# Ordering the fifth attention unit and two weight packets behind the first block's input

## Chip, cores and metric

One core of one Trainium2 chip runs the whole program. The metric is the device time of one execution in microseconds (us). TensorE (PE) does matrix products, VectorE (DVE), ScalarE (ACT) and GpSimd (POOL) work on elements, and SyncE (SP) issues most of the DMAs. Each engine works through its own instructions in a fixed order, which a scheduler has chosen when the program was built.

## What is computed

An attention with a forget gate over 4 batches, 8 heads, 576 positions and head size 64, and then two MLPs over its 2304 rows of 512, with 2048 hidden columns. All is float32; inside, most operands are split into a high part and a rest, and a product takes three terms.

```python
scores = q @ k.T / 8 + minimum(-(cum[:, None] - cum[None, :]), 0)   # cum = cumsum(maximum(s, 0))
attn = softmax(where(causal, -1e9, scores))
x = attn @ v                                       # heads side by side: (2304, 512)
x = (s * maximum(x @ w_in, 0)**2 + b) @ w_out      # first MLP
h = x @ w_in2
out = (maximum(h, 0) + alpha * minimum(h, 0)) @ w_out2
```

## The kernel before

The attention is cut into 32 units: a batch, a pair of heads, and a range of rows (0 to 319 or 320 to 575). `units` lists, for each batch, the four pairs of the first range and then the four of the second. Units 0 to 3 (`EARLY = 4`) have tiles of their own in places that weights take later. For a unit, `transpose_qk` turns q and k on VectorE (L375); `scores(u, h)` writes the bias of the gates for a head (L435 on VectorE; in the first eight units L431 on ScalarE for the second head), multiplies (sc, L457), adds and takes the minimum (L461), takes the exponential with its sum (L473), adds 1e-9 to the sum (L480), takes the reciprocal (L481) and normalizes on GpSimd (probs, L484). `values(u, h)` transposes the probabilities on TensorE (pt, L515), copies them (pf, L519), multiplies with v (av, L531) and copies the result into x (xf, L546).

The MLPs go over blocks of 256 rows (later ones of 512). A block has 16 steps `f`: `up(f)` makes 128 hidden columns (hp, L772), ScalarE and GpSimd apply the activation (L791, L793, L131), and `down(f)` adds to the block's output (acc, L886). Block 0 of the first MLP takes rows 0 to 255, so it needs units 0 to 3; `inputs(0, 0)` splits its x into xh (cast, L130) and xl (subtraction on VectorE, L131), four pieces each. In the first block the weights are made as it goes: `fetch(0, f)` loads a slice of w_in and w_out by DMA, and `packet(0, f)` brings its 64-bit numbers into float32 (`convert`: L140 on ScalarE, L141 and L142 on VectorE, for wi and for wo) and splits them (L130 on ScalarE; L131 on VectorE for the first, on GpSimd for the second). Packets 0 to 2 stand among the early units, packet 3 behind the scores of unit 2, and packet `f + 4` is asked for at step f (`AHEAD = 4`). The raw slices go into tiles that are used in turn: packet 6 takes those of packet 3, packet 7 those of packet 4.

`attention()` is a generator: each `next` writes a bit more of the attention into the program, in an order written out by hand. Before the block, the main loop calls it until `done` has reached the fourth unit, and at each step as far as `pace` says. The order of the program gives the priorities by which the scheduler, which runs a timeline of its own, fixes the order on each engine: an instruction that stands later may come first if its operands are ready earlier. `tc.issue_after(ins)` takes that freedom away: what is written inside it on the engine of `ins` comes behind `ins` on that engine.

`busy(n)` (L97) issues n products over zeros, 512 columns each, whose result is not used: 16 at the beginning, 1 after each of the early scores and values, and 4 at three places.

Of the kernel before, what the change touches and what calls it, by code (L numbers as in the profile page):

```python
# [8 lines left out]
F32 = mybir.dt.float32  # L9
# [4 lines left out]
ALU = mybir.AluOpType  # L14
# [5 lines left out]
def tile_forget_attention__then__two_mlps(  # L20
# [20 lines left out]
    nc = tc.nc  # L41
# [52 lines left out]
    def busy(n):  # L94

        for _ in range(n):
            tc.keep_in_program_order(nc.tensor.matmul(scratch, dense[:, :P], dense, start=True, stop=True))  # L97

    busy(16)
# [29 lines left out]
    def split(hi, lo, src, lo_eng=nc.vector):  # L129
        nc.scalar.copy(hi, src)  # L130
        lo_eng.tensor_tensor(out=lo, in0=src, in1=hi.bitcast(F32), op=ALU.subtract)  # L131
# [125 lines left out]
    xf = {}  # L257
# [111 lines left out]
    def transpose_qk(u):  # L369
# [4 lines left out]
        for dst, src in zip(turned, u.nats):  # L374
            nc.vector.transpose(dst, src)  # L375
# [28 lines left out]
    def scores(u, h):  # L404
# [11 lines left out]
        for r in u.blocks:  # L416
# [13 lines left out]
            if flip:  # L430
                nc.scalar.activation(  # L431
                    pt[:rows, :i1], u.cums[h][:rows, :i1], AF.Relu, scale=-1.0, bias=cumT[:rows, r, head : head + 1]
                )
            else:
                nc.vector.tensor_scalar(  # L435
                    out=pt[:rows, :i1], in0=u.cums[h][:rows, :i1], scalar1=cumT[:rows, r, head : head + 1],
                    scalar2=0.0, op0=ALU.subtract, op1=ALU.min,
                )
# [42 lines left out]
        nc.vector.reciprocal(sm[:, :nr], sm[:, :nr])  # L481
# [8 lines left out]
    def values(u, h):  # L490
# [45 lines left out]
        if u.n < EARLY:  # L536
            busy(4 if (u.n, h) == (EARLY - 1, 0) else 1)
# [24 lines left out]
    done = 0  # L562

    def attention():
# [33 lines left out]
        packet(0, 3)  # L598
        yield from alternate(scores(us[3], 0), values(us[2], 0), transpose_qk(u))
        yield from alternate(scores(us[3], 1), values(us[2], 1))  # L600
        yield from values(us[3], 0)
        last = us[3]
        for n in range(EARLY, len(units)):
# [3 lines left out]
            yield from alternate(scores(u, 0), values(last, 1))  # L607
# [22 lines left out]
    def inputs(layer, t):  # L630
# [20 lines left out]
        for c in range(NCC):  # L651
            on_pool = layer == 0 and t
            split(xh[c], xl[c], src[:, c], nc.gpsimd if on_pool else nc.vector)
# [317 lines left out]
    for f in range(AHEAD):  # L971
        packet(0, f)
    fetch(0, AHEAD + 1)

    x, late = inputs(0, 0), []
    for n in range(len(BLOCKS) * NF):
# [5 lines left out]
        if layer == 0 and t == 0 and f + AHEAD < NF:  # L982
            with tc.issue_after(relus[f - 1]) if f else nullcontext():
                packet(0, f + AHEAD)
            for g in range(f + AHEAD + 1, min(f + AHEAD + 3, NF)):
                fetch(0, g)
# [54 lines left out]
```

## Time and profile before

| | |
|---|---|
| median of 3 runs | 1041.17 us (1040.21 to 1043.41) |
| the profiled execution | 1043.1 us, its span 1041.2 us |
| busy over the span | PE 1021.4, DVE 686.3, ACT 672.7, POOL 468.1 us |
| mean granted TensorE clock | 0.993 |

The span goes from the first instruction to the last, and the times in the rows below count from its start. Busy time of PE contains the products over zeros. A granted clock of 1.00 is TensorE's upper level (2.4 GHz), 0.50 its lower one (1.2 GHz). In a timeline, a row gives start and duration of one or several like instructions (x and their count) and in brackets how long the engine stood idle before and what ended that.

### The profile page before, as it was taken

The page shows a single profiled execution, that of the slowest core. Times are in us where ns is not written, and L with a number is a line of the kernel's source. Part 1 is how long each engine was busy: PE and PEld are TensorE (multiplying, and loading weights), DVE is VectorE, ACT ScalarE, POOL GpSimd, SP SyncE. Part 2 cuts the span into 40 slices and gives each one's busy share as a digit, 9 for nine tenths or more (in the row PEclk, how much of TensorE's full clock was granted, in tenths as well). Part 3 has the DMA queues.
Part 4 walks back from the last instruction along what each step waited for, and adds up shares of the span by engine and source line. Part 5 has one row for each costly group of instructions (what it writes and reads, how often), then busy time and mean ns, then how long its engine had stood idle before and what let it go on. Part 6 is the DMA issues. An engine that isn't in the chain of part 4 may idle for free.

```text
span 1041.2 us, 20629 instructions
## 1 busy us (share of the span) xinstructions
PE 1021.4 (98%) x6952; PEld 927.0 (89%) x6952; DVE 686.3 (66%) x1605; ACT 672.7 (65%) x1669; POOL 468.1 (45%) x892
## 2 busy tenths in 40 slices
PE   9889999999999999999999999999999999999998
PEld 4568899999999999999999888998799999999996
DVE  6879875687677766667655975767775456446443
ACT  5868866777787877778776776645564455345443
POOL 5546675666677666677562100288721011001000
PEclk9889999999999999999999999999999999999999
DMA  7979533343232432234214762466654235334331
GB/s 157 268 174 252 150 63 69 69 97 72 52 84 62 90 92 52 67 68 93 64 44 145 241 201 81 124 194 200 196 178 143 98 101 179 105 95 132 107 104 55
DMA packets 197929, 125.44 MB, mean 120 GB/s; under 512 B 138496, under 2 KB 167936, under 8 KB 197824
## 3 DMA queue, kind: packets, MB, share of 16 engines
q1 hardware_dynamic: 193744, 123.56, 42.9%
q8 instruction: 55, 0.90, 0.4%
q10 hardware_dynamic: 4080, 0.57, 0.3%
q14 instruction: 50, 0.41, 0.1%
HBM read 106.19 MB, written 17.90 MB: 119 GB/s over the span
## 4 chain that ended last, share of the span: by engine, by line
PE 77%; DMA 5%; POOL 5%; ACT 4%; DVE 4%; issue 3%; SPq 1%; ACTq 0%; DVEq 0%; POOLq 0%
PE hp L772 18%; PE acc L896 16%; PE acc L886 16%; PE p L806 13%; PE pt L515 4%; PE av L531 4%; POOL sum L727 2%; PE sc L460 2%; DMA vn<-in_v_dram 1%; PE sc L459 1%; DMA sums_d<-w 1%; DMA wo<-in_moe_w_out_dram 1%; PE acc_first L97 1%; PE sc L457 1%; POOL probs L484 1%
## 5 line engine op out<-in xcount | busy, mean ns | idle before, releaser
L772 PE MATMUL hp<-xh,w 128*128 128x256 f32 (+1 forms) x1024 | 229.1, 301 | 0.5 <-ACT r L791 0.5
L896 PE MATMUL acc<-w,ring 128*128 128x512 f32 x864 | 214.1, 391 | 0.0
L896 PEld LDWEIGHTS acc<-w,ring 128*128 128x128 f32 x864 | 156.0, 188 | 27.8
L772 PEld LDWEIGHTS hp<-xh,w 128*128 128x128 f32 x1024 | 171.4, 189 | 6.6 <-ACT r L791 1.0
L886 PE MATMUL acc<-gh,w 128*128 128x256 f32 x896 | 172.3, 286 | 0.5 <-ACT res L915 0.3
L772 PE MATMUL hp<-xl,w 128*128 128x256 f32 (+1 forms) x512 | 152.6, 298 | 0.0
L886 PEld LDWEIGHTS acc<-gh,w 128*128 128x128 f32 x896 | 136.0, 189 | 3.1 <-issue 1.6
L872 POOL TENSOR_TENSOR cc<-u,t 128x256 f32<-128x256 f32 x32 | 25.9, 809 | 228.9 <-DVE u L863 198.9
L886 PE MATMUL acc<-gl,w 128*128 128x256 f32 x448 | 118.7, 288 | 2.0 <-POOL gl L131 2.0
L484 POOL TENSOR_SCALAR probs<-probs,sm 64x64 f32<-64x64 f32 (+4 forms) x160 | 91.0, 581 | 64.8 <-DVE sm L481 52.5
L473 ACT ACTIVATE probs<-probs,nm 64x64 f32<-64x64 f32 (+4 forms) x160 | 90.0, 563 | 37.8 <-DVE nm L461 25.7
L131 POOL TENSOR_TENSOR gl<-r,gh 128x256 fp32r<-128x256 f32 x112 | 89.3, 797 | 51.3 <-ACT gh L130 44.8
L806 PE MATMUL p<-xs,sums 128*128 128x256 f32 x768 | 104.4, 282 | 0.7 <-DVE u L848 0.7
L806 PEld LDWEIGHTS p<-xs,sums 128*128 128x128 f32 x768 | 97.8, 189 | 2.8 <-DVE u L848 1.2
L772 PEld LDWEIGHTS hp<-xl,w 128*128 128x128 f32 x512 | 97.1, 190 | 3.3 <-issue 0.4
L461 DVE CUSTOM_DVE_ANT_0 probs<-sc,probs 128x320 f32<-128x320 f32 (+3 forms) x160 | 68.2, 427 | 40.4 <-PE sc L460 28.0
L791 ACT ACTIVATE r<-hp 128x256 f32<-128x256 f32 (+1 forms) x144 | 58.1, 403 | 44.5 <-PE hp L772 36.9
L806 PEld LDWEIGHTS p<-xs,w 128*128 128x128 f32 x576 | 78.8, 189 | 9.0 <-DVE u L863 2.3
L806 PE MATMUL p<-xs,w 128*128 128x256 f32 x576 | 82.2, 283 | 2.4 <-DVE u L863 1.5
L886 PEld LDWEIGHTS acc<-gl,w 128*128 128x128 f32 x448 | 80.1, 189 | 4.8 <-POOL gl L131 2.6
L515 PE MATMUL pt<-ident,probs 128*128 128x128 f32 x480 | 75.0, 277 | 5.7 <-POOL probs L484 5.6
L817 DVE SCALAR_TENSOR_TENSOR ph<-pl,misc,ph 128x512 f32<-128x512 f32 x64 | 52.7, 823 | 38.2 <-ACT pl L833 38.0
(149 smaller groups left out, 2133.9 us busy)
## 6 DMA issues: line engine op xcount, KB each, us to landing
sums<-sums_d SPq DMA_DIRECT2D x128, 256.0 KB, 2.7
wi<-in_moe_w_in_dram SPq DMA_DIRECT2D x32, 512.0 KB, 5.0
wo<-in_moe_w_out_dram SPq DMA_DIRECT2D x32, 512.0 KB, 5.0
cum<-cum_d SPq DMA_DIRECT2D x32, 288.0 KB, 3.8
sums_d<-w SPq DMA_DIRECT2D x64, 128.0 KB, 1.9
cum<-cum_d SPq DMA_DIRECT2D x30, 160.0 KB, 3.2
nat<-in_k_dram SPq DMA_DIRECT2D x64, 72.0 KB, 2.5
x_d<-res SPq DMA_DIRECT2D x18, 256.0 KB, 2.2
```

The lines of the kernel that those rows point to most:

```text
L131: lo_eng.tensor_tensor(out=lo, in0=src, in1=hi.bitcast(F32), op=ALU.subtract)
L461: nc.vector.tensor_tensor_reduce(out=pt[:rows, j0:j1], in0=scr, in1=pt[:rows, j0:j1], scale=SCALE if flip else -SCALE, scalar=init, op0=AL ...
L473: nc.scalar.activation(pt[:rows, :n], pt[:rows, :n], AF.Exp, bias=nm[:rows, m : m + 1], scale=1.0 if flip else -1.0, accum_out=sm[:rows, m ...
L484: nc.gpsimd.tensor_scalar(out=probs[r][:rows, :n], in0=probs[r][:rows, :n], scalar1=sm[:rows, m : m + 1], scalar2=1.0, op0=ALU.mult, op1=A ...
L515: nc.tensor.transpose(tp[:, o : o + P], u.probs[h][r][:, k0 : k0 + P], ident)
L531: nc.tensor.matmul(av[:, nq - w : nq], lhs, part[:, o : o + w], start=(c == 0 and z == 0), stop=(c == last_c and z == len(parts) - 1), ski ...
L772: nc.tensor.matmul(hs, a[:, c], b[c], start=(n == 0), stop=(n == len(terms) * NCC - 1))
L791: relus.append(nc.scalar.activation(r, hs, AF.Relu, scale=1.0 / W_SCALE).ins)
L806: nc.tensor.matmul(bank, lhs[:, c * P : (c + 1) * P], rhs[:, c], start=(start and c == 0 and z == 0), stop=(c == 1 and z == 2), skip_group ...
L817: nc.vector.scalar_tensor_tensor(out=r, in0=u, scalar=nalpha[:, f : f + 1], in1=r, op0=ALU.mult, op1=ALU.add).ins
L886: nc.tensor.matmul(banks[d] if count == 2 else acc[d // 2][:, d % 2], a[:, d * P : (d + 1) * P], b, start=(f == 0 and (d % 2 == 0 or count ...
L896: nc.tensor.matmul(banks[m], a[:, m * P : (m + 1) * P], b, start=(f == 0 and b is woh and a is gh), stop=(f == NF - 1 and a is gl),)
```

## The change

Three things. Packet 3 leaves the attention, where it stood behind unit 2, and is written behind `inputs(0, 0)`; its VectorE instructions and those of packet 4 come behind the last subtraction of the block's x (`x_parts[-1]`) on VectorE. Unit 4's transpose and its biases on VectorE come behind the eighth reciprocal (`turns[7]`, the second head of unit 3), and in the program its transpose stands beside the last values of unit 3, its scores behind them; `done` reaches the fourth unit before unit 4's scores are written. The products over zeros are 9 in place of 16 at the beginning and 1 in place of 4 behind unit 3's first values.

```diff
--- before.py
+++ after.py
@@ -96,7 +96,7 @@
         for _ in range(n):
             tc.keep_in_program_order(nc.tensor.matmul(scratch, dense[:, :P], dense, start=True, stop=True))
 
-    busy(16)
+    busy(9)
 
     def load_constants():
         nc.sync.dma_start(out=gate_s, in_=act_s.partition_broadcast(P))
@@ -128,7 +128,7 @@
 
     def split(hi, lo, src, lo_eng=nc.vector):
         nc.scalar.copy(hi, src)
-        lo_eng.tensor_tensor(out=lo, in0=src, in1=hi.bitcast(F32), op=ALU.subtract)
+        return lo_eng.tensor_tensor(out=lo, in0=src, in1=hi.bitcast(F32), op=ALU.subtract).ins
 
 
     def convert(raw, wt):
@@ -254,7 +254,7 @@
                 op0=ALU.mult,
             )
 
-    xf = {}
+    xf, x_parts = {}, []
 
     def x_block(t):
         if t not in xf:
@@ -372,7 +372,8 @@
         nq = u.q1 - u.q0
         turned, *u.qk = qk_tiles(u, F32, "turned")
         for dst, src in zip(turned, u.nats):
-            nc.vector.transpose(dst, src)
+            with behind_early(u):
+                nc.vector.transpose(dst, src)
         yield
         if u.native:
             return
@@ -432,10 +433,11 @@
                     pt[:rows, :i1], u.cums[h][:rows, :i1], AF.Relu, scale=-1.0, bias=cumT[:rows, r, head : head + 1]
                 )
             else:
-                nc.vector.tensor_scalar(
-                    out=pt[:rows, :i1], in0=u.cums[h][:rows, :i1], scalar1=cumT[:rows, r, head : head + 1],
-                    scalar2=0.0, op0=ALU.subtract, op1=ALU.min,
-                )
+                with behind_early(u):
+                    nc.vector.tensor_scalar(
+                        out=pt[:rows, :i1], in0=u.cums[h][:rows, :i1], scalar1=cumT[:rows, r, head : head + 1],
+                        scalar2=0.0, op0=ALU.subtract, op1=ALU.min,
+                    )
             nc.gpsimd.affine_select(
                 out=pt[:rows, i0:i1], in_=pt[:rows, i0:i1], pattern=[[-1, rows]], base=0,
                 channel_multiplier=1, compare_op=ALU.is_ge,
@@ -478,7 +480,7 @@
         if u.n == 0:
             busy(4)
         nc.vector.tensor_scalar(out=sm[:, :nr], in0=sm[:, :nr], scalar1=1e-9, scalar2=None, op0=ALU.add)
-        nc.vector.reciprocal(sm[:, :nr], sm[:, :nr])
+        turns.append(nc.vector.reciprocal(sm[:, :nr], sm[:, :nr]).ins)
         for m, r in enumerate(u.blocks):
             rows, n = IB[r][1] - IB[r][0], IB[r][1]
             nc.gpsimd.tensor_scalar(
@@ -534,7 +536,7 @@
                         skip_group_check=True,
                     )
         if u.n < EARLY:
-            busy(4 if (u.n, h) == (EARLY - 1, 0) else 1)
+            busy(1)
         t0 = u.b * S + q0
         while t0 < u.b * S + q1:
             t = t0 // T
@@ -559,7 +561,10 @@
                 else:
                     gens.remove(g)
 
-    done = 0
+    done, turns = 0, []
+
+    def behind_early(u):
+        return tc.issue_after(turns[2 * EARLY - 1]) if u.n == EARLY else nullcontext()
 
     def attention():
         nonlocal done
@@ -595,16 +600,18 @@
         u = Unit(EARLY)
         load_qk(u), load_cum(u), load_v(u)
         yield from alternate(scores(us[2], 1), values(us[1], 1))
-        packet(0, 3)
-        yield from alternate(scores(us[3], 0), values(us[2], 0), transpose_qk(u))
+        yield from alternate(scores(us[3], 0), values(us[2], 0))
         yield from alternate(scores(us[3], 1), values(us[2], 1))
         yield from values(us[3], 0)
+        yield from alternate(values(us[3], 1), transpose_qk(u))
+        done = EARLY
+        yield
         last = us[3]
         for n in range(EARLY, len(units)):
             nxt = Unit(n + 1) if n + 1 < len(units) else None
             if nxt:
                 load_qk(nxt)
-            yield from alternate(scores(u, 0), values(last, 1))
+            yield from alternate(scores(u, 0), *([values(last, 1)] if n > EARLY else []))
             done = n
             if last.native and last.n >= EARLY:
                 load_v(u)
@@ -650,7 +657,7 @@
             )
         for c in range(NCC):
             on_pool = layer == 0 and t
-            split(xh[c], xl[c], src[:, c], nc.gpsimd if on_pool else nc.vector)
+            x_parts.append(split(xh[c], xl[c], src[:, c], nc.gpsimd if on_pool else nc.vector))
         return xh, xl
 
     def wide_inputs(t, first):
@@ -968,11 +975,11 @@
     side = attention()
     while done < reached(0):
         next(side)
-    for f in range(AHEAD):
-        packet(0, f)
+    x, late = inputs(0, 0), []
+    with tc.issue_after(x_parts[-1]):
+        packet(0, AHEAD - 1)
     fetch(0, AHEAD + 1)
 
-    x, late = inputs(0, 0), []
     for n in range(len(BLOCKS) * NF):
         (layer, t), f = BLOCKS[n // NF], n % NF
         if f == 0:
@@ -980,7 +987,7 @@
             goal, x = reached(min(t + 1, NB - 1)) if layer == 0 else len(units), None
         late.append((down, finish, f, up(f)))
         if layer == 0 and t == 0 and f + AHEAD < NF:
-            with tc.issue_after(relus[f - 1]) if f else nullcontext():
+            with tc.issue_after(relus[f - 1] if f else x_parts[-1]):
                 packet(0, f + AHEAD)
             for g in range(f + AHEAD + 1, min(f + AHEAD + 3, NF)):
                 fetch(0, g)
```

## Rows read from the trace of the kernel before

**Rows 1.** Stretches of 20 us: PE, PEld, DVE, ACT, POOL busy; clock; DMA.

```profile
40.00:60.00 20.00, 16.20 (x66) 10.51 (x65) 16.30 (x47) 14.15 (x38) 12.07 (x19) 0.76 1.05 263
...
800.00:820.00 20.00, 20.00 (x128) 18.14 (x127) 8.71 (x16) 7.84 (x19) 1.47 (x2) 1.00 0.31 105
```

**Rows 2.** Timeline of TensorE, 55 to 65 us.

```profile
55.70 0.90 PE L515 MATMUL pt<-ident,probs 128*128 128x128 f32 x3 [2.79 <-POOL probs L484]
56.40 2.23 PE L531 MATMUL acc_first<-pf,vn 128*128 128x320 f32 x6
58.42 1.91 PE L97 MATMUL acc_first<-dense 128*128 128x512 bf16 x4
...
62.96 1.30 PE L531 MATMUL av<-pf,vn 128*128 128x320 f32 x6
...
64.13 0.47 PE L772 MATMUL hp<-xh,w 128*128 128x256 f32 x1
```

**Rows 3.** Timeline of VectorE, 45 to 66.5 us.

```profile
45.93 0.47 DVE L461 CUSTOM_DVE_ANT_0 probs<-sc,probs 128x320 f32<-128x320 f32 x1
...
46.34 1.66 DVE L142 SCALAR_TENSOR_TENSOR wt<-wo,wt 128x512 uint32<-128x512 uint32 x1
...
49.78 1.03 DVE L375 STREAM_TRANSPOSE turned<-nat 128x832 f32<-128x832 f32 x1
...
53.54 0.25 DVE L480 TENSOR_SCALAR sm<-sm 128x3 f32<-128x3 f32 x1
...
54.30 0.16 DVE L481 RECIPROCAL sm<-sm 128x3 f32<-128x3 f32 x1
...
65.92 0.51 DVE L131 TENSOR_TENSOR xl<-xf,xh 128x256 fp32r<-128x256 f32 x1 [0.56 <-ACT xh L130]
```

**Rows 4.** Timeline of ScalarE and GpSimd, 47 to 61 us.

```profile
47.28 1.70 POOL L484 TENSOR_SCALAR probs<-probs,sm 128x192 f32<-128x192 f32 x2
...
48.03 0.62 ACT L130 CAST w<-wt 128x512 fp32r<-128x512 f32 x1 [0.74 <-DVE wt L142]
...
48.55 0.56 ACT L473 ACTIVATE probs<-probs,nm 128x320 f32<-128x320 f32 x1
...
54.64 1.52 POOL L484 TENSOR_SCALAR probs<-probs,sm 64x64 f32<-64x64 f32 x3
...
60.59 0.58 ACT L519 COPY pf<-pt 128x512 f32<-128x512 f32 x1 [1.45 <-PE pt L515]
```

**Rows 5.** Groups by line on VectorE, 43.8 to 58.3 us: count, busy us, mean ns.

```profile
L142 DVE SCALAR_TENSOR_TENSOR wt<-wo,wt 128x512 uint32<-128x512 uint32 x2 | 2.3, 1168 | 0.0
...
L141 DVE TENSOR_SCALAR wt<-wt 128x512 uint32<-128x512 uint32 x4 | 2.0, 501 | 0.0
...
L142 DVE SCALAR_TENSOR_TENSOR wt<-wi,wt 128x512 uint32<-128x512 uint32 x2 | 1.4, 678 | 0.0
L131 DVE TENSOR_TENSOR w<-wt,w 128x512 fp32r<-128x512 f32 x2 | 1.3, 664 | 0.0
```

**Rows 6.** Groups by line on TensorE, 47.4 to 66.4 us.

```profile
L457 PE MATMUL sc<-turned 64*128 64x448 f32 (+2 forms) x12 | 4.2, 471 | 0.6 <-DVE turned L375 0.6
```

**Rows 7.** The first block as one stretch, columns as in rows 1.

```profile
66.40:140.00 73.60, 72.30 (x479) 61.31 (x478) 66.64 (x137) 58.46 (x141) 48.94 (x72) 1.00 0.68 170
```

**Rows 8.** Groups by line on TensorE, 66 to 140 us.

```profile
L772 PE MATMUL hp<-xl,w 128*128 128x256 f32 x53 | 15.3, 288 | 0.0
```

**Rows 9.** Timeline of SP's queue, unit 5's q and k.

```profile
50.84 1.98 SPq L327 DMA_DIRECT2D nat<-in_q_dram  x4
52.86 4.79 SPq L327 DMA_DIRECT2D nat<-in_k_dram  x4
```

**Rows 10.** Timeline of the beginning, 0 to 15 us, all engines.

```profile
1.31 5.72 PE L97 MATMUL acc_first<-dense 128*128 128x512 bf16 x16 [1.31 <-POOL dense L77]
...
14.28 1.15 ACT L431 ACTIVATE probs<-cum,cumT 64x64 f32<-64x64 f32 x3 [0.56 <-DMA cum<-cum_d]
```

**Rows 11.** A stretch of the lower clock, columns as in rows 1.

```profile
53.40:60.20 6.80, 4.50 (x14) 3.08 (x15) 4.59 (x15) 3.03 (x8) 5.49 (x9) 0.50 0.97 194
```

## The prediction

> **What bounds the kernel now.** I read the busy time by stretch first, then the order of instructions on TensorE, VectorE, ScalarE and GpSimd ahead of the first block, and last what the first block has to spare. Late in the kernel TensorE is busy 20.00 of 20 us at the full clock, and its work there is the bound [rows 1]. A change can gain only where TensorE is idle, runs at the lower clock or multiplies zeros. All three lie at the beginning: from 40 to 60 us it is busy 16.20 of 20 us at a mean clock of 0.76 [rows 1]. The first block's products (hp, L772) begin only at 64.13 us [rows 2]. What brings them forward is worth nearly its whole length, less the TensorE work that was done meanwhile and then comes later.
>
> **Who holds the first block up.** Its x needs all of units 0 to 3, and the second head of unit 3 is last. Its largest exponential (128x320) ends at 48.55 + 0.56 = 49.11 us on ScalarE; yet VectorE adds the 1e-9 to its sum at 53.54 and takes the reciprocal from 54.30 to 54.46 [rows 3, 4]. In those 4.4 us VectorE does, in its fixed order, merges and subtractions of packets 3 and 4, unit 4's transpose (1.03 us) and its biases; the transpose stands for them [rows 3]. TensorE stands idle for 2.79 us ahead of the transposes at 55.70, until GpSimd's L484 has the scores normalized [rows 2]. The exponential itself was late: its minimum was done at 45.93 + 0.47 = 46.40 us, but ScalarE had packet 3's cast (L130) in front of it, which waited 0.74 us for a merge of 1.66 us on VectorE [rows 3, 4].
>
> **The change, part by part.**
>
> *Packets 3 and 4 and unit 4 leave the stretch ahead of the reciprocal.* VectorE's part of the two packets is L142 2.3 + 1.4, L141 2.0, L131 1.3: 7.0 us [rows 5]. Without them the exponential follows its minimum at about 46.5 and ends at 47.1; the two small instructions on the sum take at most 0.25 and 0.16 us, so the reciprocal ends near 47.6 and not at 54.46, 6.9 us earlier. GpSimd can't follow by all of it: it normalizes unit 3's first head until 47.28 + 1.70 = 48.98 us [rows 4], so the last head's L484 starts there in place of 54.64: **5.7 us** earlier. That is the first term.
>
> *From L484 to x.* Before, from the end of L484 (54.64 + 1.52 = 56.16) to the end of the last xl (65.92 + 0.51 = 66.43) went 10.3 us [rows 3, 4]. The chain alone needs less: six transposes, of which three took 0.90 us at the lower clock, so about 0.9 us at the full one; the copy of 0.58 us; and the 3.5 us from the start of unit 3's last values at 62.96 to 66.43: 5.0 us [rows 2 to 4]. Between them TensorE did the first head's values (2.23 us) and four products over zeros (1.91 us), both at the lower clock, and the scores of unit 4's second head, half of the 4.2 us that unit 4's scores take [rows 2, 6]. Three of the four zero products go: 1.91 x 3/4 = 1.4 us for certain. If the scores fall elsewhere and the clock holds, it is 10.3 - 5.0 = 5.3 us. TensorE's order isn't prescribed for the scores, and pauses remain that may lower the clock; I take the middle, 3.3 us. **x is ready 5.7 + 3.3 = 9.0 us earlier** (bounds 7.1 and 11.0), at about 57.4 us.
>
> *What comes back.* Before x was ready TensorE had done all of unit 4's scores, 4.2 us [rows 6]. Unit 4's transpose now waits for the reciprocal alone, so about half of them fit into the 10 us in which x is finished, and some 2 us come later. VectorE gets the packets' 7.0 us into the first block, where it is busy 66.64 of 73.6 us from 66.4 to 140 us [rows 7]. What it has to spare, 7.0 us, is just what is moved in: the cost is 0 if every gap can be filled and 7.0 us if none can. The two returns are on different engines and overlap, so the larger counts; nothing in the rows is nearer to one end, and I take the middle, **3.5 us**.
>
> The merge at L142, which reads two tensors, takes 0.68 us, and 1.66 us at 46.34, where GpSimd normalizes at 47.28 [rows 3 to 5]. By the Trainium skill (GPSIMD Engine Reference, section Key points) GpSimd shares its SBUF interfaces with VectorE, whose instructions with two SBUF inputs contend with it; the trace agrees. It speaks against moving merges into the block, where GpSimd is busy 48.94 of 73.6 us [rows 7]: three more of the four at 1.66 us would raise the return by 2.9 us, and 2.6 us would be gained in place of 5.5.
>
> *Lead of the weights.* Three packets stand ready at the block's start, not five. Four hp<-xl products make a step, 53 of them stand in 74 us, so a step takes 5.6 us [rows 8]. Packet 3 is needed at the fourth, 17 us on, and its VectorE share is 3.5 us. Cost 0; if a step finds no packet, each late one costs that 3.5 us. Packets 6 and 7 are loaded into the tiles that 3 and 4 leave, so their DMAs move back on SP's queue or hold up what stands behind them: unit 5's eight loads of q and k, at 50.84 and 52.86 us [rows 9]. I take 0, since steps 6 and 7 are 34 us off; the price if not is a rival below.
>
> *Nine zero products at the beginning.* Sixteen run from 1.31 to 7.03 us; seven fewer free TensorE by up to 5.72 x 7/16 = 2.5 us earlier. It reaches no further than ScalarE's bias at 14.28 us, which waits for the DMA of the cumulated gates [rows 10], and nothing that TensorE does starts that DMA. I take 0; bounds are 2.5 us of gain and, if TensorE gets one more spell at the lower clock, like 6.8 us from 53.4 us on [rows 11], half of it, 3.4 us of loss.
>
> **Sum.** 9.0 - 3.5 = 5.5 us. The profiled execution took 1043.1 us, 1.9 us more than its span of 1041.2; with the change 1037.6. It stands 1.9 us above the median of the runs, 1041.17, so against the median 1041.2 - 5.5 = **1035.7 us**. Nothing later takes it back, as TensorE is full there whatever came before [rows 1].
>
> **Rivals.**
>
> *VectorE takes it all back in the block (within 0.3%).* For it: with 66.64 + 7.0 of 73.6 us it has nothing left [rows 7]. Against it: by the code the last packet is asked for at the twelfth of 16 steps, and VectorE is relieved from there on. Low bound of the gain and full return: 7.1 - 7.0 = 0, 1041 us. 0.20.
>
> *The clock.* Ten zero products are gone, and the last units run alone, in short pieces with pauses. A spell at half the clock began at 53.4 us, after TensorE had gone idle, and lasted 6.8 us [rows 11]. If one covers the block's first products, dense work loses half of that: 5.5 - 3.4 = 2.1 gained, 1039 us. Against it: that spell is there before too, and is likelier moved than added. The Trainium skill (TensorE: Matmul & The Clock Gate, section Why this matters for your kernels) says that pauses between bursts of products return the engine to its lower clock; this spell agrees. 0.06.
>
> *Slower.* SP issues in order. If packet 6's load stands ahead of unit 5's, those wait until packet 3 is converted, near 57.4 + 3.5 = 61 us. Their issue takes from 50.84 to 57.65, 6.8 us [rows 9], so it ends near 68, 10 us behind x. Unit 5's transpose and scores come 3 us later still. Meanwhile TensorE has unit 4's values and the first two steps, at half a step's 5.6 us each some 6 us, and idles for 7; with unit 6 late by half as much, 9.0 - 3.5 - 10.5 = -5: 1046 us. It decides from loads that end some 6 us behind x. Against it: unit 5's tile is free as soon as unit 4 is transposed, long before. 0.08.
>
> *More.* Both engines fill their gaps and the chain runs at its shortest: 11.0 - 1 = 10 us, 1031 us. 0.11.
>
> **Chances and range.** The forecast (3.1 to 9 us gained) has 0.55, more 0.11, the return 0.20, the clock 0.06, slower 0.08. The measurement tells about 0.3%, 3.1 us, from no change: faster 0.66, same 0.26, slower 0.08. The range goes from 1030.5 to 1041.5 us: above it lie the slower case and some half of the return, below it next to nothing.
>
> **What the profile would show.** Right: the reciprocal of unit 3's second head near 47.6 us, with nothing of packets 3 and 4 or of unit 4 ahead of it on VectorE; its L484 near 49; the last xl and dense hp products near 57; VectorE over 95% busy in the block. Wrong: dense hp products at 62 us or later; TensorE waiting between x and 140 us for weights (w) or for VectorE and GpSimd by more than 7 us; or new idle time later.

## The result, and the profile after

The changed kernel took 1050.07 us (median of 6 runs, 1046.48 to 1053.97), the kernel before, run beside it, 1041.45 us: ratio 1.0098, 95% interval [1.0077, 1.012]. It is 8.6 us slower; 1035.7 had been forecast, with a range up to 1041.5. The first profiled execution took 1046.48 us, the least of the six. A second, of the same kernel unchanged, is among the experiments.

Line numbers behind L375 are shifted: L375 is L376 after, L457 L459, L461 L463, L481 L483, L484 L486, L515 L517, L772 L779.

Up to x the profile reads much as forecast. The rows on VectorE that answer to [rows 3]:

```profile
48.67 0.18 DVE L483 RECIPROCAL sm<-sm 128x3 f32<-128x3 f32 x1
49.04 1.04 DVE L376 STREAM_TRANSPOSE turned<-nat 128x832 f32<-128x832 f32 x1 [0.20 <-DMA vn<-in_v_dram]
...
58.42 0.42 DVE L131 TENSOR_TENSOR xl<-xf,xh 128x256 fp32r<-128x256 f32 x1 [1.76 <-ACT xh L130]
58.77 1.43 DVE L141 TENSOR_SCALAR wt<-wt 128x512 uint32<-128x512 uint32 x4
60.11 0.48 DVE L463 CUSTOM_DVE_ANT_0 probs<-sc,probs 128x320 f32<-128x320 f32 x1
60.52 0.08 DVE L463 DVE_READ_ACCUMULATOR2_ANT nm<- 128x1 f32 x1
60.52 1.04 DVE L376 STREAM_TRANSPOSE turned<-nat 128x832 f32<-128x832 f32 x1
61.48 0.65 DVE L142 SCALAR_TENSOR_TENSOR wt<-wi,wt 128x512 uint32<-128x512 uint32 x1
...
65.71 0.47 DVE L463 CUSTOM_DVE_ANT_0 probs<-sc,probs,nm 128x256 f32<-128x256 f32 x1
...
72.72 1.26 DVE L482 TENSOR_SCALAR sm<-sm 128x2 f32<-128x2 f32 x1
73.89 0.68 DVE L142 SCALAR_TENSOR_TENSOR wt<-wo,wt 128x512 uint32<-128x512 uint32 x1
74.50 0.15 DVE L483 RECIPROCAL sm<-sm 128x2 f32<-128x2 f32 x1
```

And on GpSimd, answering to [rows 4]:

```profile
49.01 1.21 POOL L486 TENSOR_SCALAR probs<-probs,sm 64x64 f32<-64x64 f32 x3 [1.00 <-DVE sm L483]
```

The eighth reciprocal (unit 3's second head) starts at 48.67 us in place of 54.30, its L486 at 49.01 in place of 54.64, and x is ready at 58.84 in place of 66.43. The new thing stands below that: the tenth reciprocal, of unit 4's second head, comes at 74.50 us. TensorE shows why that counts (timeline, as in [rows 2]):

```profile
56.89 0.47 PE L779 MATMUL hp<-xh,w 128*128 128x256 f32 x1
...
58.35 1.23 PE L459 MATMUL sc<-turned 64*128 64x320 f32 x4
...
75.80 0.33 PE L517 MATMUL pt<-ident,probs 128*128 128x128 f32 x1 [1.64 <-POOL probs L486]
```

The last scores of unit 4's second head are multiplied at 58.35, behind the first of x's products. The head then needs 16 us to its reciprocal: on VectorE it waits behind unit 5's transpose and the packets' L141 and L142, and its last maximum is at 65.71 though its scores were there at 59.58. ScalarE takes up its last exponential only at 70.24, 4.1 us behind that maximum: ahead of it stand two conversions of a packet (L140), each waiting for its DMA, the block's activations and an exponential of unit 5.

```profile
70.24 0.77 ACT L475 ACTIVATE probs<-probs,nm 128x576 f32<-128x576 f32 x1
```

In the kernel before the same scores stood at 61.80, ahead of x's products, and the reciprocal at 65.20, ahead of unit 5's transpose:

```profile
61.80 1.24 PE L457 MATMUL sc<-turned 64*128 64x320 f32 x4
...
65.20 0.17 DVE L481 RECIPROCAL sm<-sm 128x2 f32<-128x2 f32 x1
...
66.36 1.03 DVE L375 STREAM_TRANSPOSE turned<-nat 128x832 f32<-128x832 f32 x1
```

How the span divides at x (the end of the last xl) and at block 1's first step (ScalarE's first operation on its products; busy time as in [rows 1]; PE, PEld, DVE, ACT, POOL, clock, DMA). Before:

```profile
0.00:66.43 66.43, 59.06 (x243) 33.91 (x243) 48.92 (x163) 42.64 (x121) 36.52 (x114) 0.90 0.85 211
66.43:152.43 86.00, 84.70 (x577) 73.59 (x577) 74.50 (x160) 68.96 (x170) 59.91 (x98) 1.00 0.63 156
```

After, and the stretch right behind x and one late in the kernel:

```profile
0.00:58.84 58.84, 52.98 (x222) 30.06 (x223) 38.27 (x146) 38.65 (x114) 31.34 (x110) 0.94 0.85 203
58.84:155.94 97.10, 91.93 (x598) 79.15 (x596) 82.29 (x176) 72.61 (x176) 64.21 (x100) 0.96 0.57 158
...
58.80:100.00 41.20, 38.01 (x236) 32.47 (x235) 41.00 (x77) 32.23 (x74) 25.73 (x29) 0.92 0.82 236
800.00:820.00 20.00, 20.00 (x127) 18.11 (x127) 8.93 (x17) 8.71 (x20) 1.47 (x2) 1.00 0.34 109
```

x is 7.6 us earlier, but from x to block 1's first step it is 97.10 us and not 86.00. Those 11.1 us are idle TensorE, 97.10 - 91.93 = 5.17 against 1.30 (3.9 us); two spells at the lower clock, 6.8 us (3.4 us lost); and, as what is left, 3.8 us of more work. That is 598 products against 577: four scores and eight transposes of unit 4, which the kernel before did ahead of x, and eleven of the block's output (acc), which it did behind block 1's first step, less two of av. So the first step comes 3.5 us later, and the span ends 3.5 us later (1044.7 against 1041.2). In all 20 profiles of this study the end is 887 to 892 us behind block 1's first step: all but these 5 us are decided ahead of it.

### The profile page after: what moved, and what is told of

It reads as the page before. It is cut to its first block, busy times and chain, and to the rows that moved or that the text cites. A ratio compares the mean times of both kernels' runs of the same rounds, so it can differ in the third digit from the quotient of the medians.

```text
span 1044.7 us, 20584 instructions
## 1 busy us (share of the span) xinstructions
PE 1021.6 (98%) x6942; PEld 927.5 (89%) x6942; DVE 679.2 (65%) x1605; ACT 672.5 (64%) x1669; POOL 470.4 (45%) x892
## 4 chain that ended last, share of the span: by engine, by line
PE 78%; DVE 6%; DMA 6%; ACT 4%; POOL 3%; issue 3%; SPq 1%; ACTq 0%; DVEq 0%; POOLq 0%
PE hp L779 19%; PE acc L893 17%; PE acc L903 16%; PE p L813 12%; PE pt L517 4%; PE av L533 4%; PE sc L462 2%; DMA sums_d<-w 2%; PE sc L461 2%; DMA wo<-in_moe_w_out_dram 1%; POOL sum L734 1%; DVE wt L142 1%; DMA wi<-in_moe_w_in_dram 1%; DVE w L131 1%; DVE wt L141 1%
## 5 line engine op out<-in xcount | busy, mean ns | idle before, releaser
L779 PE MATMUL hp<-xh,w 128*128 128x256 f32 (+1 forms) x1024 | 229.8, 301 | 1.0 <-ACT r L798 1.0
L779 PEld LDWEIGHTS hp<-xh,w 128*128 128x128 f32 x1024 | 171.5, 190 | 9.2 <-ACT r L798 1.4
L779 PE MATMUL hp<-xl,w 128*128 128x256 f32 (+1 forms) x512 | 152.5, 298 | 0.0
L486 POOL TENSOR_SCALAR probs<-probs,sm 64x64 f32<-64x64 f32 (+4 forms) x160 | 91.8, 587 | 59.0 <-DVE sm L483 53.0
L779 PEld LDWEIGHTS hp<-xl,w 128*128 128x128 f32 x512 | 97.1, 190 | 2.7
L463 DVE CUSTOM_DVE_ANT_0 probs<-sc,probs 128x320 f32<-128x320 f32 (+3 forms) x160 | 68.2, 428 | 46.0 <-PE sc L462 30.5
L517 PE MATMUL pt<-ident,probs 128*128 128x128 f32 x480 | 74.5, 277 | 6.0 <-POOL probs L486 4.8
```

The source lines that it names most:

```text
L463: nc.vector.tensor_tensor_reduce(out=pt[:rows, j0:j1], in0=scr, in1=pt[:rows, j0:j1], scale=SCALE if flip else -SCALE, scalar=init, op0=AL ...
L486: nc.gpsimd.tensor_scalar(out=probs[r][:rows, :n], in0=probs[r][:rows, :n], scalar1=sm[:rows, m : m + 1], scalar2=1.0, op0=ALU.mult, op1=A ...
L517: nc.tensor.transpose(tp[:, o : o + P], u.probs[h][r][:, k0 : k0 + P], ident)
L779: nc.tensor.matmul(hs, a[:, c], b[c], start=(n == 0), stop=(n == len(terms) * NCC - 1))
```

## The experiments

The theories, by the names that the expectations use. **A**: the moved packets fill VectorE in the first block, so the attention of units 4 to 7 falls behind. **B**: with fewer zero products TensorE's clock is low at the beginning. **C**: unit 4's wait for the eighth reciprocal holds the attention up. **D**: it is where unit 4 is written, behind the packets. **E**, **F**: the order fixed when the kernel is built, on VectorE (E, packets pass the heads of units 4 to 7) or on TensorE (F, the block's steps pass them). **G**: unit 4's second head, and not x, sets the pace. (The tenth reciprocal is that of unit 4's second head.)

The kernel before was run beside each group of runs, with medians from 1039.83 to 1041.45 us. Differences between medians of different groups can therefore be off by 1 to 2 us; the ratios are the better measure.

All runs in one table: kernel, zeros at the beginning, median (range, runs) in us, ratio to the kernel before with its interval, and from the profile when x was ready, when block 1 began, and the mean ns of a zero product (L97) between 7 and 30 us.

| run | zeros | us | ratio | x | block 1 | ns |
|---|---|---|---|---|---|---|
| before | 16 | 1041.45 (1040.21 to 1043.53, 6) | 1 | 66.43 | 152.43 | 384 |
| after | 9 | 1050.07 (1046.48 to 1053.97, 6) | 1.0098 [1.0077, 1.012] | 58.84 | 155.94 | 467 |
| e16 after again | 9 | 1053.28 (1) | | 63.70 | 161.81 | 622 |
| e1 zeros alone | 9 | 1056.87 (1055.44 to 1059.08, 4) | 1.0158 [1.0141, 1.0175] | 72.69 | 163.49 | 621 |
| e2 unit 4 alone | 16 | 1046.07 (1041.03 to 1050.71, 6) | 1.0052 [1.0027, 1.0077] | 66.27 | 153.98 | 524 |
| e3 packets alone | 16 | 1039.91 (1036.37 to 1045.77, 10) | 0.9989 [0.997, 1.0007] | 57.13 | 147.83 | 384 |
| e4 after | 16 | 1052.61 (1051.45 to 1055.41, 4) | 1.0124 [1.0105, 1.0143] | 58.09 | 161.87 | 384 |
| e5 scores first | 9 | 1051.57 (1049.28 to 1053.79, 4) | 1.0107 [1.008, 1.0135] | 60.53 | 157.53 | 534 |
| e6 less on VectorE | 9 | 1051.81 (1049.16 to 1055.31, 4) | 1.0107 [1.0075, 1.0138] | 68.19 | 161.52 | 622 |
| e7 packets alone | 9 | 1048.75 (1046.48 to 1049.67, 4) | 1.0072 [1.0053, 1.0091] | 59.61 | 156.98 | 534 |
| e8 packets alone, denser | 16 | 1043.6 (1039.03 to 1045.32, 10) | 1.0025 [1.0009, 1.0041] | 58.74 | 151.91 | 389 |
| e9 two behind | 9 | 1049.56 (1047.09 to 1055.07, 4) | 1.0096 [1.0058, 1.0134] | 65.32 | 162.69 | 543 |
| e10 VectorE held | 9 | 1050.25 (1046.57 to 1051.28, 6) | 1.0092 [1.0065, 1.0118] | 63.60 | 158.95 | 621 |
| e11 VectorE held | 16 | 1046.76 (1043.23 to 1053.17, 12) | 1.0066 [1.0047, 1.0086] | 57.62 | 154.61 | 384 |
| e12 packets alone, held | 16 | 1039.67 (1036.63 to 1043.32, 12) | 0.9994 [0.9972, 1.0015] | 59.10 | 148.18 | 384 |
| e13 TensorE held | 9 | 1054.94 (1052.62 to 1056.98, 4) | 1.0134 [1.0118, 1.015] | 63.60 | 161.08 | 621 |
| e14 TensorE held | 16 | 1046.69 (1045.55 to 1048.87, 5) | 1.0059 [1.0047, 1.0072] | 58.08 | 157.40 | 384 |
| e15 all three held | 16 | 1043.05 (1040.9 to 1047.92, 11) | 1.0019 [1, 1.0038] | 58.14 | 152.91 | 384 |
| e17 all three held | 9 | 1050.02 (1048.83 to 1050.88, 4) | 1.0101 [1.0081, 1.0121] | 61.10 | 156.02 | 599 |
| e18 and packets 3, 4 | 16 | 1048.2 (1047.0 to 1054.25, 6) | 1.0088 [1.0066, 1.011] | 57.72 | 157.71 | 384 |

### The three parts one by one

e1: the kernel before with the zeros of the one after.

```diff
-    busy(16)
+    busy(9)
...
-            busy(4 if (u.n, h) == (EARLY - 1, 0) else 1)
+            busy(1)
```

> The kernel before with the zero products alone changed (9 for 16 at the beginning, 1 for 4 behind unit 3's first values). Theory A (the moved packets fill VectorE in the first block, the attention of units 4 to 7 falls behind and the second block's x comes late): no change, 1038 to 1045 us. Rival B (fewer zero products let TensorE's clock fall): most of the loss is here, 1047 us or more, with spells at half the clock that the kernel before doesn't have.

e2: unit 4's part alone (packet 3 back behind unit 2, packets free on VectorE, zeros as before).

```diff
+            with behind_early(u):
...
+        yield from alternate(values(us[3], 1), transpose_qk(u))
```

> Unit 4's part alone: its transpose and biases behind the eighth reciprocal, its scores written behind the fourth unit; packets 3 and 4 and the zero products as before. Theory A: VectorE gets no packets into the block, so it isn't slower: 1035 to 1042 us, with the transposes of units 6 and 7 no later than 83 and 105 us. Rival C (unit 4's new place itself holds the attention up): 1046 us or more, units 6 and 7 late as in the changed kernel (93 and 119 us).

e3: the packets' part alone (unit 4 and the zeros as before). e4: the changed kernel with 16 and 4 zeros.

```diff
-        packet(0, 3)
...
+    with tc.issue_after(x_parts[-1]):
+        packet(0, AHEAD - 1)
...
+            with tc.issue_after(relus[f - 1] if f else x_parts[-1]):
```

> The packets' part alone: 3 and 4 written behind the first block's x and put behind its last subtraction on VectorE; unit 4 and the zero products as before. Theory A: the loss is here, 1045 to 1054 us, VectorE over 97% busy for 40 us from the block's start, units 6 and 7 transposed late. Rival C: no loss, 1036 to 1043 us.

> The changed kernel with 16 and 4 zero products again. Theory A: as slow as the changed kernel, 1046 to 1054 us. Rival B: as the kernel before or better, 1036 to 1043 us.

The packets alone cost nothing, 1039.91, and x is ready at 57.13: A falls as a cause by itself. The zeros alone cost 1.6% (some 16 us) and unit 4's part alone 0.5%. The time of e2 is what C expected, but its profile doesn't show a late attention: from x to block 1 it takes 87.71 us, 1.7 more than before, and its x gains nothing (66.27), with a spell at the lower clock from 10.7 to 20.9 us. But putting the zeros back into the changed kernel doesn't help, 1052.61: the parts don't add up. What they do together has to be looked for.

### Where unit 4 is written, VectorE's load, the zeros with the packets

e5: unit 4's first scores written ahead of x. e6: VectorE's second half of the conversion of packets 3 and 4 left out (the weights of these two packets lack it). e7: e3 with the zeros of the changed kernel. e8: e3 with two zero products per score in units 0 and 1.

```diff
# e5
-        done = EARLY
-        yield
+        yield from scores(u, 0)
+        done = EARLY
# e6
+        if short:
+            return
         nc.vector.tensor_scalar(out=wt, in0=wt, scalar1=3,
# e8
-                    busy(1)
+                    busy(2 if u.n < 2 else 1)
```

> The changed kernel, with unit 4's first scores written ahead of the block's x and of packets 3 and 4, as before the change; its transpose and biases still wait for the eighth reciprocal. Theory D (unit 4 is written behind the packets, so the scheduler lets their VectorE work pass unit 4, and with it units 5 to 7): most of the return is gone, unit 4's second reciprocal within 12 us of its first (19 in the changed kernel), unit 6 transposed before 87 us; 1035 to 1044 us. Rival C (the wait for the eighth reciprocal itself): as slow as the changed kernel, 1046 us or more.

> The changed kernel without the shift and the merge (L141, L142) of packets 3 and 4 on VectorE: their weights keep only what ScalarE's L140 gives. It takes 4 x 0.4 + 4 x 0.7 = 4.4 us or more off VectorE in the block. If VectorE's load is what holds the attention up (theories A and D): unit 4's second reciprocal some 4 us earlier at least, and 4 to 10 us faster than the changed kernel, 1040 to 1046 us. If the written order or the wait matters and not the load (C): less than 2 us from the changed kernel's 1050.

> The changed kernel without unit 4's part: packets 3 and 4 behind x, 9 and 1 zero products, unit 4 as before. D and C: no return beyond some 3 us, so 1036 to 1043 us, unless TensorE stays at half the clock at the beginning. Theory B (9 zero products leave TensorE at the lower clock for the first 20 to 30 us in most executions): 8 to 16 us slower than the same kernel with 16 (1039.9), so 1047 to 1056 us.

> The packets' part alone (e3_packets), with 2 zero products in place of 1 behind each score of units 0 and 1. Theory B (whether TensorE keeps its clock at the beginning decides between fast and slow executions of one kernel): the clock holds, runs lie closer together and lower, 1034 to 1040 us. If the clock at the beginning doesn't matter: as e3_packets, 1036 to 1046 us, or slower by the added products.

e5 gains nothing (D falls). e6 takes eight passes over weights off VectorE and gains nothing in the time either, but it doesn't settle A: its x came late, at 68.19 us, in another order, and from x to block 1 it took 93.33 us, where the changed kernel's profiles have 97.10 and 98.11. e7 loses 8.8 us against e3, with unit 4 as before, so C is not needed for the loss. e8 is 3.7 us slower than e3, although its granted clock stayed at 1.00 from 6.9 to 82.0 us: the clock ahead of x isn't all.

### The order that the engines were given

Each engine works in the order fixed when the kernel was built, so the orders can be read side by side. How many of the first block's 16 steps TensorE starts ahead of turning each head's probabilities (units 4 to 7, two heads each), and how many packets VectorE has merged ahead of each head's reciprocal:

```text
          TensorE: steps ahead of the head     VectorE: packets ahead of the reciprocal
before    0  2  3  5  7 10 12 14               5  5    7    9   10   13   15   15.5
e3        0  3  5  7  9 12 13 15               3  5    8   11   12   14.5 15.5 15.5
e1        0  1  2  4  6  8 10 13               5  5    6    8   10   12   13   15
after     1  5  7 10 11 13 14 16               3  7    8.5 12.5 14   15.5 15.5 15.5
e7        1  5  7 10 11 13 14 16               3  7    8.5 12.5 14   15.5 15.5 15.5
e4        1  5  7 10 12 14 14 16               3  7    9   13   15   15.5 15.5 15.5
e15       1  2  3  5  7 10 12 14               3  5    7    9   10   13   15   15.5
```

After, e4, e5 and e7 share one picture: five steps (before: two) and seven packets (before: five) stand ahead of unit 4's second head, and the heads behind it follow late. e7 gets it through the zeros alone. That is what the next runs test: they hold packets or steps where the kernel before has them.

e9: packets 5 and 6 behind unit 4's second reciprocal on VectorE. e10: all packets from 5 on, as before. e11: the same with 16 zeros. e12: the same in e3.

```diff
+                at = {1: 9, 2: 9, 3: 10, 4: 10, 5: 11, 6: 12, 7: 12, 8: 12, 9: 13, 10: 13, 11: 14}.get(f, 99)
+                with tc.issue_after(turns[at]) if at < len(turns) else nullcontext():
                     packet(0, f + AHEAD)
```

> The kernel after, with the packet work of packets 5 and 6 on VectorE put behind the second reciprocal of unit 4 (the tenth). E (VectorE's order, written down when the kernel is compiled, lets packets 5 and 6 and then each later one pass a reciprocal of units 4 to 7): the tenth reciprocal comes at 66 to 70 us in place of 74.50, but packets 7 to 15 still pass the later ones, so unit 7 is turned after 112 us and the kernel takes 1044 to 1050. A (the sum of VectorE's work from x to 100 us): 1047 to 1052, unit 7 turned at 119 as before. B (the zeros at the beginning): 1047 to 1052 as well.

> The kernel after, with every packet from 5 to 15 put behind the reciprocal that it stands behind in the kernel before's order on VectorE (5 and 6 behind the tenth, 7 and 8 behind the eleventh, 9 behind the twelfth, 10 to 12 behind the thirteenth, 13 and 14 behind the fourteenth, 15 behind the fifteenth). E: unit 5 to 7 turned at about 60, 81 and 103 us, the last part of block 1's x near 145, and the kernel takes 1035 to 1041. A: the same VectorE work in the same time; TensorE waits for weights in place of probabilities, block 1's x stays near 152 and the kernel takes 1046 to 1052. B: nine zeros are still there, 1044 to 1050.

> The same pinned order with the 16 and 4 zero products of the kernel before. E alone: within 3 us of the pinned kernel with nine. E with B: 1032 to 1038 and 5 us or more under the pinned kernel with nine, and block 1's x at about 143. A: 1048 to 1054, as with 16 zeros and the free order.

> The packets' part alone (16 and 4 zeros, unit 4 written as before) with the pinned order. E: the free order of this kernel lets a packet pass here and there (twelfth reciprocal behind packet 10, fourteenth behind packet 14's first half), so a gain of 0 to 3 us on it: 1035 to 1040. A: no change, 1038 to 1042; if the pinned packets come too late for TensorE, its waits for weights grow by over 2 us from x to 140 us and the kernel takes 1040 to 1044.

With nine zeros VectorE's order brings nothing (1050.25); with 16 it brings 5.9 us (1052.61 to 1046.76). e9 missed: the tenth reciprocal came at 77.18 us; x itself came only at 65.32, and behind it the head still took 11.9 us, where the first profile of the changed kernel has 15.7. In e12 the order makes no difference (1039.67 against 1039.91 in e3): there the heads were hardly passed.

e13: the steps held on TensorE alone. e14: with 16 zeros. e15: with 16, and the packets held on ScalarE and VectorE too. e16: the changed kernel again.

```diff
+        at = {2: 9, 3: 10, 5: 11, 7: 12, 10: 13, 12: 14, 14: 15}.get(f) if n < NF else None
+        with tc.issue_after(pts[at]) if at in pts else nullcontext():
             late.append((down, finish, f, up(f)))
```

> The kernel after, with steps 2, 3, 5, 7, 10, 12 and 14 of the first block put, on TensorE alone, behind the turning of the probabilities that each stands behind in the kernel before (the second head of unit 4, then each head of units 5, 6 and 7 in turn); nothing else is held. F (TensorE's order, written down when the kernel is compiled, lets four steps of the block pass unit 4's second head, because x's products now stand ahead of that head's scores): the tenth reciprocal at 66 to 70 us, unit 7 turned near 105, the last part of block 1's x at 144 to 148, the kernel 1039 to 1045. A (VectorE is full whatever the order) or E (VectorE's order): TensorE merely waits at the held steps, block 1's x at 150 or later, 1047 to 1052. B (nine zeros): 1046 to 1050.

> The same with the 16 and 4 zero products of the kernel before. F: block 1's x at 142 to 146, the kernel 1036 to 1041, some 11 us under the changed kernel with 16 zeros and the free order. F with B: this one 3 to 8 us under the one with nine zeros. A or E: 1047 to 1053.

> As the one before, and the packets from 5 on also behind the exponentials (on ScalarE) and the reciprocals (on VectorE) of the heads that they stand behind in the kernel before. F: the same within 3 us, since TensorE's order sets the rest; E: over 3 us less than with TensorE's order held alone.

> The kernel after, unchanged, for a second profiled execution. F: the same order, so the tenth reciprocal 15 to 16 us behind x and unit 7 turned 59 to 61 us behind it, whatever the clock at the beginning. B: a time above the first profile's by about half of what the clock is longer at its lower level ahead of x.

With 16 zeros, TensorE's order alone brings 5.9 us too, where F had expected some 11, and all three together 9.6 (1052.61 to 1043.05). With nine, TensorE's order alone costs 4 to 5 us (1054.94), more than any theory expected: F, too, is no sufficient cause there. e16's profile gives the reason why nine differ. Its stretches, as above:

```profile
0.00:63.70 63.70, 61.07 (x222) 33.24 (x223) 40.20 (x146) 38.96 (x114) 33.22 (x110) 1.00 0.79 186
63.70:161.81 98.11, 92.97 (x598) 80.07 (x596) 82.28 (x175) 72.68 (x177) 64.00 (x100) 0.95 0.58 157
```

The same 222 products take 61.07 us up to x, where the first profile had 52.98. The zero products between 7 and 30 us (groups by line: count, busy us, mean ns) tell the clock. In e16:

```profile
L97 PE MATMUL acc_first<-dense 128*128 128x512 bf16 x19 | 9.9, 622 | 0.0
```

In the kernel before:

```profile
L97 PE MATMUL acc_first<-dense 128*128 128x512 bf16 x26 | 8.4, 384 | 0.0
```

A product of the same shape takes 622 against 384 ns: e16 is at 1.2 GHz until 30.6 us, where its record of the granted clock has its first change (ahead of it the rows show 1.00). x comes 4.9 us later than in the first profile, the end 6.6 us later. B had expected half of the longer time at the lower clock, which is some 18 us, so 9: not all of it reaches the end. From x on the two agree: 98.11 and 97.10 us to block 1, and 15.6 and 15.7 us to the tenth reciprocal.

### The zeros at an order held, and packets 3 and 4

e17: e15 with nine zeros and one. e18: e15 with packets 3 and 4 behind unit 4's second head on ScalarE and VectorE.

```diff
# e17
-    busy(16)
+    busy(9)
# e18
+        if n == 0:
+            with tc.issue_after(turns[9]), tc.issue_after(exps[9]):
+                packet(0, 3)
+                packet(0, 4)
```

> The kernel with all three engines held, with nine zero products at the beginning and one later, in place of 16 and 4. B (with nine the clock stays at its lower level at the beginning in most executions, as it did till 30.5 us in the changed kernel's second profile, whose x came 4.4 us and whose end came 6.6 us later than in its first): 4 to 9 us over the kernel with 16, so 1047 to 1052, and the profile shows the products of the first 30 us at twice the duration. If the zeros matter only through the order that the compiled kernel gets: within 2 us of it, 1041 to 1045.

> The kernel with all three engines held and 16 zeros, and packets 3 and 4, too, behind the second head of unit 4 on ScalarE and VectorE (with all held and packets 3 and 4 free, the first six of their eight VectorE passes ran between 58 and 64 us, and the last maximum of that head, whose scores were ready at 58.9, came at 65.06). G (the second head of unit 4, not x, sets the pace of the first block, and the change put it behind x and behind the moved packets): its reciprocal at 62 to 65 in place of 68.87, the third step's square before 74 in place of 77.94, the last part of block 1's x at 141 to 144, the kernel 1036 to 1041. A (the first block's VectorE work as a whole): the packets come late in their place, the block waits for weights, 1042 to 1046.

e17 is 7.0 us above e15 by the medians, and 0.82% by the ratios. The orders are close, though not equal behind unit 5 (e17: 6, 8, 10, 13 steps ahead of the last four heads). From x to block 1 it takes as long, 94.92 against 94.77 us; x is 3.0 us later, and 2.9 us come behind the first step, where its record has one more spell of 3.4 us (1.7 us lost). Its zero products from 7 to 30 us:

```profile
L97 PE MATMUL acc_first<-dense 128*128 128x512 bf16 x20 | 10.1, 599 | 0.0
```

And its first stretch:

```profile
0.00:61.10 61.10, 58.38 (x222) 32.02 (x223) 40.03 (x146) 38.87 (x114) 32.94 (x110) 0.83 0.80 195
```

In e15 the order of before is there, and x 8.3 us earlier, and yet block 1 begins 0.5 us later. TensorE's timeline in e15, with its scores ahead of and behind the wait:

```profile
57.64 1.23 PE L459 MATMUL sc<-turned 64*128 64x320 f32 x4
...
70.87 0.33 PE L517 MATMUL pt<-ident,probs 128*128 128x128 f32 x1 [3.33 <-POOL probs L486]
71.12 2.29 PE L459 MATMUL sc<-turned 64*128 64x320 f32 x4
```

The held third step waits with TensorE 3.33 us for unit 4's second head, and behind that wait the clock is granted at half from 71.1 to 77.9 us: the same four scores take 2.29 us and not 1.23. G said that this head sets the pace. e18 brought its reciprocal forward as expected:

```profile
62.12 0.17 DVE L483 RECIPROCAL sm<-sm 128x2 f32<-128x2 f32 x1
```

but the kernel takes 1048.2 us, 5.2 more than e15 and more than either theory expected. TensorE now waits for the block's own steps:

```profile
74.02 0.74 PE L894 MATMUL acc<-gh,w 128*128 128x256 f32 x4 [2.17 <-ACT gh L130]
75.61 0.58 PE L894 MATMUL acc<-gl,w 128*128 128x256 f32 x1 [0.85 <-POOL gl L131]
...
78.96 0.48 PE L517 MATMUL pt<-ident,probs 128*128 128x128 f32 x1 [1.27 <-POOL probs L486]
```

The cast of the last part of block 1's x began at 142.87 us, but three steps of the first block were still to begin (at 143.73, 146.91 and 151.67 us). So G falls too: with the head first, the steps are late; with the steps first, the heads are.

## Why the prediction was wrong

In one line, the forecast was 9.0 - 3.5 = 5.5 us of gain. The first profile of the changed kernel has 7.6 - 11.1 = -3.5, the second 2.7 - 12.1 - 0.7 = -10.1 (the last term behind block 1's first step). The median of the six runs, 8.6 us of loss, lies between.

**The chain to x** held in the first profile. The first term, L484 5.7 us earlier, measured 54.64 - 49.01 = 5.6. From there to x the forecast took off 3.3 us; the kernel took off 7.6 - 5.6 = 2.0, within the bounds. x came 7.6 us earlier and not 9.0; in the second profile, at the lower clock until 30.6 us, only 2.7.

**"What comes back, 3.5 us"** is the first step that failed: 11.1 us came back in the first profile, 12.1 in the second, beyond the bound of 7.0. The forecast let the returns on TensorE and on VectorE overlap and counted the larger. In the profile they add up: 3.8 us of products, 3.9 us of idle and 3.4 us of lower clock. The forecast knew that part of unit 4's scores would come later, but priced them as 2 us of TensorE's work. What it missed is the chain behind them: the scores of unit 4's second head, which stood ahead of x before, now stand behind x's first products; that head's maxima, exponentials and sum then queue among the packets, and every later head is late too, their reciprocals by 3.6 to 14.5 us. The size was about right for what it named: with the packets moved and those scores still ahead of x, 4.7 and 3.1 us came back (e3 and e12, from x to block 1 90.70 and 89.08 us).

The 20 profiles agree with this reading, without being a test of it: it takes both, moved packets and late scores. Where the last four scores of that head begin ahead of x's first product (before, e1, e3, e8, e12), x to block 1 takes 86.0 to 93.2 us. Where they begin behind it, 94.8 to 103.8, but for e2, which leaves the packets in their old place (87.7), and e6, which leaves out much of their work on VectorE (93.3).

How far the order alone is the cause depends on the zeros. With 16 it is shown: holding the old order on three engines gives back 9.6 us. With nine it gives nothing in the time (1050.07 and 1050.02). So either of the two, nine zeros or the free order, is enough for the loss: putting back the zeros alone (e4, 1052.61) or the order alone (e17, 1050.02) gains nothing, and only both together (e15, 1043.05) give back 7.0 of the 8.6 us. With nine, the order's gain is hidden, although the way from x to block 1 gets 2 to 3 us shorter. In the held order 94.8 us of e15 against 86.0 before remain, of which 3.33 us are one wait and 3.4 us the lower clock behind it. Why no order tried brings that stretch under 89 us with x near 58 us stays open; e18 shows only that this wait can't be had for nothing. So x was not the bound that the forecast took it for: a large part of its lead was work put off.

**"Nine zero products, 0"** is the second. Six pairs differ in the zeros alone by the code. Nine cost some 16 us (e1), 8.8 (e7 against e3), 8.3 (e13 against e14), 7.0 (e17 against e15) and 3.5 (e10 against e11); after against e4 they cost nothing (-2.5). Most of these pairs also got another order from the scheduler. In e13 and e14 the steps and the packets stand alike at all eight heads (1 2 3 5 7 10 12 14 and 3 7 7 9 10 13 15 15.5), and TensorE's products between x and block 1 come in nearly the same order: this is the cleanest price, 8.3 us by the medians and 0.75% by the ratios, over twice the bound of 3.4. The zero products take 621 ns in e13 and 384 in e14, and x comes at 63.60 in place of 58.08. The bound took one spell of 6.8 us; in the changed kernel's second profile it is some 25 us at the lower clock. Between after and e4 the price is hidden: e4's order, in which still more steps pass the heads, keeps TensorE idle for 103.78 - 93.37 = 10.4 us behind x.

Together: by the ratios e17 and e15 put 0.82 of the 0.98% on the zeros (e13 and e14 0.75), and e15, 1.0019 [1, 1.0038] of the kernel before, leaves some 2 us of loss to the moved packets and unit 4, in place of the 5.5 us to be gained. That sum stands on a held order, and e17's isn't quite that of e15; in the free one the shares can't be told apart.

**The rivals.** "VectorE takes it all back" saw the right place: VectorE was busy 41.00 of 41.20 us behind x. But its load alone is not the cause: e3 has the packets there too, VectorE busy 77.80 of 90.70 us, without a loss.

```profile
57.13:147.83 90.70, 88.23 (x595) 77.48 (x593) 77.80 (x170) 71.48 (x177) 66.90 (x101) 0.98 0.63 169
```

The merges that were moved weren't slowed to 1.66 us either: packets 3 and 4 have theirs at 61.48 to 64.64 us, at 0.65 to 0.68 each. "The clock" named the right mechanism for a spell in the block and priced it well (3.4 us), but looked for it there alone. "Slower" by SP's queue fell: unit 5 was turned at 60.52 us, earlier than the 66.36 of before. **Lead of the weights** held: TensorE waited for no packet from x to 100 us; its two waits there were for unit 4's probabilities (1.6 us) and unit 6's transpose (1.5 us).

No version tried is measurably faster than the kernel before; e3 and e12 are the same within their intervals.

## What to carry to other kernels

A start that comes earlier is worth only the idle time that it removes: list what the engine did meanwhile and where that goes, and take the time at the next point that everything waits for (here block 1's first step), not at the point that was moved. Before pricing a small edit, compare the orders that the engines are given; a scheduler that follows its own timeline can turn a few zero products into another order hundreds of instructions on. Price products that keep the clock up by the executions in which it stays low, and look at more than one profile.

## What was not expected of the hardware

The clock at the beginning isn't the same in every execution of one kernel. With 16 zero products (1.31 to 7.03 us) the granted clock rose to 2.4 GHz at 4.9 to 7.2 us in all nine profiles (e8, with products added, left aside), and the zero products between 7 and 30 us took 384 ns in eight of them (524 in e2). With nine (to 5.33 us) it rose at 4.2 to 5.9 us in four of ten profiles and fell again at 7.6 to 9.3 us in each; TensorE stood idle there for at most 0.15 us between. In the other six it rose only at 20.8 to 30.7 us, though TensorE was busy for over 28 of the 28.7 us from 1.31 to 30; the mean was 467 to 622 ns in all ten. The Trainium skill (TensorE: Matmul & The Clock Gate, section What's actually happening) says that the number of products at the lower clock differs between runs of one kernel; two profiles of the changed kernel agree, 5.9 and 30.6 us, and by more than that section lets one expect.

A pause of 3.33 us on TensorE in the middle of dense work (e15, until 70.87 us) was followed by 6.8 us at 1.2 GHz. TensorE was busy throughout these, so by an estimate the pause cost 3.33 + 3.4 us, about twice its length.
